# Attention scores on four quarters of the TensorE array, in a kernel of retention attention and two feed-forward layers

## The chip, the core and the metric

One core of one Trainium2 chip runs the whole program. The metric is the device time of one execution in microseconds (us), as the median of the runs. The engines that matter are TensorE (PE in the profile; its weight loads are PEld), VectorE (DVE), ScalarE (ACT), GpSimd (POOL) and SyncE (SP), whose queue issues most transfers.

## The reference

For each of 4 batches and 8 heads there are 576 positions with 64 features. Scores between queries and keys are multiplied by a decay that falls with the distance and is zero ahead of the query, and then by the values:

```python
scores = scale * np.matmul(q, k.transpose(0, 1, 3, 2))
gamma = 1.0 - 2.0 ** (-5.0 - np.arange(H))
Dmat = np.where(rel >= 0, gamma[:, None, None] ** rel[None, :, :], 0.0)
ret = scores * Dmat[None, :, :, :]
x = np.matmul(ret, v)                    # then (2304 tokens, 512)
h = x @ w_in;  x = (np.maximum(h, 0) + alpha * np.minimum(h, 0)) @ w_out
h = x @ w_in2; y = (h / (1 + np.exp(-1.702 * h))) @ w_out2
```

Both feed-forward layers are 512 to 2048 to 512 over 2304 tokens. All is computed in float32.

## The kernel before, in words

The attention works on 16 pairs of heads, one after the other. A pair has its two heads on the two halves of the partitions: features 0 to 63 of head `e` = 0 on partitions 0 to 63, of head 1 on 64 to 127 (`halves`, L300). The 576 positions are four chunks of 128 and a tail of 64. Since the decay is a power of the distance, only the scores inside a chunk are formed; what lies before a chunk comes in through a 64 by 64 state for each head.

For pair `i`, TensorE does five things, in this order, which the loop from L950 writes out by hand:

- `a_scores(i)` (L363): for each chunk `j` and head `e`, keys (64 by 128, the weights) times queries (64 by 128, moving), into the bank `t[e]` of the tile `sc`. Two PSUM banks are used, one for each head; three of them rotate. VectorE multiplies them by the decay table in `a_evac(i)` (L385).
- `a_outer(i)`: the states of the chunks, from scaled keys (`kts`) and values, into `st`. ScalarE scales these keys in `a_keys` (L317), once they have landed from HBM.
- `a_within(i-1)`: values times decayed scores of the pair before, into `av`.
- `a_tail(i)`: the scores of the tail, into `st`.
- `a_across(i-1)`: the states times queries of the pair before, into the same `av`.

All of these go through the helper `mm` (L353), so that they share one line in the profile and are told apart by the tile that they write: `sc`, `st` or `av`. An instruction that has 64 rows of weights uses one half of the array's rows, one with 64 columns one half of its columns. In the profile's notation rows*columns, the scores are 64*128, `a_outer` and `a_within` 128*64, `a_tail` and `a_across` 64*64 (there on two of the four quarters, head 0 on the upper left and head 1 on the lower right).

Each float32 product of the program stands in the trace as two weight loads and two matmuls: 8 products of scores in a pair are x16.

Loads: `a_load(i+4)` is issued on SP's queue at the end of pair `i`, when the buffer of an older pair is free: 864 KB of queries, keys and values (tile `ld`) and 256 KB of keys in the other layout (tile `kts`). Pieces of the first layer's weights (tile `raw`, 512 KB each) are issued between them, at times that a list of events sets in units of pairs (`row`, `at`, `run_to`). ScalarE and VectorE then work on these weights between the attention's own work, in the order in which the program was written: `w_sat` (L133), `w_range` (L137), `w_top` (L141) and, on VectorE, `w_low` (L148). Each engine runs its list in order.

The feed-forward layers that follow take TensorE from 66.5 us to the end. They are not touched.

Of the kernel before, what the change touches and what calls it, by code (L numbers as in the profile page):

```python
# [46 lines left out]
def kernel(  # L47
# [252 lines left out]
    halves = (slice(0, 64), slice(64, 128))  # L300
# [51 lines left out]
    def mm(out, lhsT, rhs, start, stop):  # L352
        return nc.tensor.matmul(  # L353
            out=out, lhsT=lhsT, rhs=rhs, start=start, stop=stop, skip_group_check=True
        )
# [7 lines left out]
    def a_scores(i, chunks=range(4)):  # L363
        q, k = ld[i][0:2]
        if i not in sc_t:
            sc_t[i] = [aps.tile([128, 512], F32, tag="sc", name="sc", bufs=3) for _ in halves]
        t = sc_t[i]
        for j in chunks:
            for e, o in enumerate(halves):
                mm(t[e][:, j * 128:j * 128 + 128], k[j][o], q[j][o], j == 0, True)  # L370

    def a_tail(i):
        q, k = ld[i][0:2]
# [552 lines left out]
    with tc.manual_schedule():  # L926
# [24 lines left out]
        for i in range(n_a + 1):  # L951
            j = i - 1
            if i < n_a:
                a_scores(i)
                a_queries(i)
                a_evac(i)
# [84 lines left out]
        for r in range(R):  # L1041
            z = r * 2 * NU
            for j in range(NJ):
                u = z + 7 * j
                for t, what in (
# [3 lines left out]
                    if r == 0 and j in (5, 6) and what in ("g22", "g12"):  # L1049
                        t = 8.01  # L1050
# [114 lines left out]
```

## Time and profile before

| what | value |
|---|---|
| median of 3 runs (lowest to highest) | 801.3 us (800.87 to 804.2) |
| the profiled execution | 800.28 us, of which its span is 798.6 us |
| PE busy in the span | 793.6 us (99%) |
| DVE, ACT busy | 642.1 us (80%), 527.9 us (66%) |
| granted TensorE clock | 1.00 in every stretch listed |
| HBM traffic | 267 GB/s over the span |

The chain of waits goes back from the last instruction to what released each; its rows in order of time give a start, a duration and the work, in us. In a matmul group, the shape rows*columns is that of the weights and the next one that of the moving operand. A matmul's own duration is longer than the distance between two starts, since they are pipelined: rates are read from a stage's duration divided by its instructions.

### The profile page before, as it was taken

What the parts mean: (1) busy time and instruction counts of PE and PEld (TensorE: products, weight loads), DVE (VectorE), ACT (ScalarE), POOL (GpSimd) and SP (SyncE); (2) the same over time, 40 slices, a digit from 0 to 9 for tenths busy, and PEclk for the clock granted to TensorE, in tenths of its full rate; (3) what the DMA queues carried; (4) which work ended last, traced back from release to release, by engine and by line L of the source; (5) the groups of instructions that cost most, each with busy time, mean ns of one, the idle gap of its engine ahead of it and who ended that gap; (6) DMA issues with size and microseconds to landing.
All of it is one profiled execution on the core that took longest, in us unless ns stands there. A gap on an engine that the chain in (4) does not pass through costs nothing.

```text
span 798.6 us, 14132 instructions
## 1 busy us (share of the span) xinstructions
PE 793.6 (99%) x5004; PEld 740.2 (93%) x5004; DVE 642.1 (80%) x1195; ACT 527.9 (66%) x959; POOL 83.5 (10%) x104
## 2 busy tenths in 40 slices
PE   9999999999999999999999999999999999999998
PEld 8998888888888888999999999999999999999997
DVE  7888987888467576879999899799677898787775
ACT  7689869885536856556678666676566675666552
POOL 2230112100022003626100000000000000000000
PEclk9999999999999999999999999999999999999999
DMA  9998999755889966797989556986435985536771
GB/s 351 417 386 333 327 352 342 286 217 209 294 278 401 360 224 227 253 337 254 337 323 355 177 174 233 343 295 235 147 125 193 323 312 187 159 120 232 267 278 60
DMA packets 87789, 214.08 MB, mean 268 GB/s; under 512 B 7971, under 2 KB 43811, under 8 KB 79014
## 3 DMA queue, kind: packets, MB, share of 16 engines
q1 hardware_dynamic: 80784, 187.99, 65.6%
q0 software_dynamic: 6784, 25.17, 9.0%
q8 instruction: 39, 0.64, 0.3%
q14 instruction: 32, 0.26, 0.1%
q10 hardware_dynamic: 150, 0.02, 0.0%
HBM read 152.59 MB, written 60.56 MB: 267 GB/s over the span
## 4 chain that ended last, share of the span: by engine, by line
PE 98%; DMA 1%; DVE 0%; issue 0%
PE acc L696 33%; PE h L696 25%; PE acc L555 16%; PE h L514 16%; PE av L353 4%; PE sc L353 2%; PE st L353 2%; DMA ws<-sm 1%; PE wps L942 0%; PE dq L326 0%; DVE c L178 0%; DVE wz L930 0%
## 5 line engine op out<-in xcount | busy, mean ns | idle before, releaser
L108 DVE TENSOR_TENSOR gsf<-g,gsf 128x384 fp32r<-128x384 f32 (+1 forms) x272 | 156.4, 586 | 54.5 <-ACT gsf L103 53.1
L103 ACT ACTIVATE gsf<-g 128x384 fp32r<-128x384 f32 (+1 forms) x272 | 145.8, 542 | 75.6 <-PE acc L696 32.8
L555 PE MATMUL acc<-gsf,wo 128*128 128x512 f32 x576 | 138.2, 389 | 0.0
L514 PE MATMUL h<-x,wi 128*128 128x512 f32 x576 | 138.2, 389 | 0.0
L696 PE MATMUL acc<-gsf,ws 128*128 128x384 f32 x768 | 135.1, 334 | 0.2 <-DMA ws<-sm 0.2
L696 PEld LDWEIGHTS acc<-gsf,ws 128*128 128x128 f32 x768 | 133.2, 188 | 0.5 <-ACT x L103 0.5
L555 PEld LDWEIGHTS acc<-gsf,wo 128*128 128x128 f32 x576 | 108.1, 188 | 22.8 <-ACT raw L103 0.3
L514 PEld LDWEIGHTS h<-x,wi 128*128 128x128 f32 x576 | 108.1, 188 | 22.5
L696 PE MATMUL acc<-x,ws 128*128 128x384 f32 x660 | 128.3, 334 | 0.0
L696 PEld LDWEIGHTS acc<-x,ws 128*128 128x128 f32 x660 | 115.5, 188 | 0.2 <-ACT tm L103 0.2
L696 PE MATMUL h<-x,ws 128*128 128x384 f32 x540 | 107.7, 334 | 0.0
L696 PE MATMUL h<-gsf,ws 128*128 128x384 f32 x576 | 101.9, 334 | 0.0
L696 PEld LDWEIGHTS h<-gsf,ws 128*128 128x128 f32 x576 | 100.0, 188 | 0.2 <-issue 0.2
L696 PEld LDWEIGHTS h<-x,ws 128*128 128x128 f32 x540 | 94.8, 188 | 0.0
L178 DVE TENSOR_TENSOR tm<-h,tm 128x384 f32<-128x384 f32 x97 | 53.6, 553 | 26.9 <-PE h L696 21.5
L178 DVE TENSOR_TENSOR g<-g 128x384 f32<-128x384 f32 x114 | 63.0, 553 | 0.7
L103 ACT ACTIVATE tm<-acc 128x384 f32<-128x384 f32 x62 | 30.4, 491 | 48.0 <-PE acc L696 46.4
L522 DVE SCALAR_TENSOR_TENSOR g<-g,rise_sb,h 128x512 f32<-128x512 f32 (+1 forms) x49 | 36.4, 742 | 29.7 <-ACT g L527 29.5
L527 ACT ACTIVATE g<-h 128x512 f32<-128x512 f32 (+1 forms) x49 | 29.1, 593 | 40.5 <-PE h L514 39.9
L178 DVE TENSOR_TENSOR raw<-raw 128x256 f32<-128x256 f32 x116 | 45.6, 433 | 1.0
L148 DVE SCALAR_TENSOR_TENSOR raw<-raw 128x1024 int32<-128x1024 int32 x32 | 39.3, 1229 | 2.6 <-ACT raw L141 2.6
L129 POOL DMA_DIRECT2D raw<-in_w_dram x44 | 23.2, 534 | 173.2 <-DVE raw L178 52.9
(104 smaller groups left out, 922.9 us busy)
## 6 DMA issues: line engine op xcount, KB each, us to landing
ws<-sm SPq DMA_DIRECT2D x32, 1024.0 KB, 7.0
ws<-sp SPq DMA_DIRECT2D x24, 1024.0 KB, 5.5
raw<-in_w_dram POOLq DMA_DIRECT2D x44, 512.0 KB, 7.5
sm<-raw SPq DMA_DIRECT2D x32, 512.0 KB, 4.3
pad<-rg SPq DMA_DIRECT2D x48, 256.0 KB, 2.7
ld<-in_qkv_dram SPq DMA_DIRECT2D x13, 864.0 KB, 7.9
raw<-in_w_dram SPq DMA_DIRECT2D x20, 512.0 KB, 8.9
r<-raw SPq DMA_DIRECT2D x16, 512.0 KB, 2.9
```

Source lines behind the costliest of these rows:

```text
L103: return nc.scalar.activation(out=out, in_=in_, func=ACTF.Copy)
L108: latest[0] = eng.tensor_tensor(out=out, in0=a, in1=b.bitcast(F32), op=ALU.subtract)
L129: eng.dma_start(out=raws[key][:, c * DM:c * DM + DM], in_=f[:, c * DM:c * DM + DM])
L148: latest[0] = nc.vector.scalar_tensor_tensor(out=g[:, 0:2 * DM], in0=t[:, :, 1], scalar=3, in1=t[:, :, 0], op0=ALU.logical_shift_left, op1 ...
L178: latest[0] = (eng or nc.vector).tensor_tensor(out=out, in0=x, in1=y, op=op)
L353: return nc.tensor.matmul(out=out, lhsT=lhsT, rhs=rhs, start=start, stop=stop, skip_group_check=True)
L514: nc.tensor.matmul(out=t, lhsT=w[:, cw, k * 128:k * 128 + 128], rhs=x[:, cx], start=(i == 0), stop=(i == 3 * NK - 1),)
L522: nc.vector.scalar_tensor_tensor(out=g[0], in0=g[1], scalar=rise_sb[:, m:m + 1], in1=h, op0=ALU.mult, op1=ALU.add)
L527: nc.scalar.activation(out=out, in_=in_, func=ACTF.Relu, scale=-1.0)
L555: nc.tensor.matmul(out=acc[0][d], lhsT=w[:, d // 2, cw, d % 2 * 128:d % 2 * 128 + 128], rhs=g[:, cx], start=(m == m0 and i == 0), stop=(m ...
L696: nc.tensor.matmul(out=out, lhsT=w(cw), rhs=x(cx), start=(start and n == 0), stop=True, skip_group_check=True,)
```

## The change

The weights of each score product are cut into two halves of 64 keys (`h`). Half `h` writes partitions `h` of the bank `t[e]` that held all 128 keys before. A score product then uses one quarter of the array: rows by the head `e`, columns by the half `h`. A chunk has four products where it had two, and each streams the same 128 queries.

```diff
         for j in chunks:
-            for e, o in enumerate(halves):
-                mm(t[e][:, j * 128:j * 128 + 128], k[j][o], q[j][o], j == 0, True)
+            for h in halves:
+                for e, o in enumerate(halves):
+                    mm(t[e][h, j * 128:j * 128 + 128], k[j][o, h], q[j][o], j == 0, True)
```

On TensorE, around the scores of a pair in the middle of the attention, this stood before (the shape is that of the output; `av<-r,ld` with 64x64 ends `a_across`, `st<-ld,kts` is `a_outer`, `av<-r,ld` with 64x128 is `a_within`, the last `st<-ld` is `a_tail`):

```order
L353 MATMUL av<-r 64x128 x6
L353 MATMUL av<-r 64x64 x2
L353 MATMUL av<-r,ld 64x64 x2
L353 MATMUL sc<-ld 128x128 x8
L353 MATMUL st<-ld,kts 64x64 x8
L353 MATMUL av<-r,ld 64x128 x8
L353 MATMUL st<-ld 64x64 x2
```

and this stands now:

```order
L353 MATMUL av<-r 64x128 x6
L353 MATMUL av<-r 64x64 x2
L353 MATMUL av<-r,ld 64x64 x2
L353 MATMUL sc<-ld 64x128 x16
L353 MATMUL st<-ld,kts 64x64 x8
L353 MATMUL av<-r,ld 64x128 x8
L353 MATMUL st<-ld 64x64 x2
```

The eight products became sixteen of half the output, in the same place; nothing around them moved.

Inside a pair the two heads take turns. With the numbers of the tiles, the scores of one pair (`sc_524` for head 0, `sc_525` for head 1) and what stands behind them were, before:

```order
L353 MATMUL sc_524<-ld_342 128x128
L353 MATMUL sc_525<-ld_342 128x128
L353 MATMUL sc_524<-ld_342 128x128
L353 MATMUL sc_525<-ld_342 128x128
L353 MATMUL st_539<-ld_342,kts_127 64x64 x8
```

The last two chunks of a pair and what stands behind them are now, with other numbers of the tiles (`sc_572` for head 0, `sc_573` for head 1):

```order
L353 MATMUL sc_572<-ld_366 64x128
L353 MATMUL sc_573<-ld_366 64x128
L353 MATMUL sc_572<-ld_366 64x128
L353 MATMUL sc_573<-ld_366 64x128
L353 MATMUL sc_572<-ld_366 64x128
L353 MATMUL sc_573<-ld_366 64x128
L353 MATMUL sc_572<-ld_366 64x128
L353 MATMUL sc_573<-ld_366 64x128
L353 MATMUL st_595<-ld_366,kts_127 64x64 x8
```

The heads alternate as before, and the two products of one head that are nearest are the two halves of one chunk's keys. On DVE, ACT, POOL and SP the instructions and their order are unchanged.

## Rows read from the trace of the kernel before

**Rows 1.** The page: busy time of TensorE, and the chain that ended last.

```profile
PE 793.6 (99%) x5004; PEld 740.2 (93%) x5004; DVE 642.1 (80%) x1195; ACT 527.9 (66%) x959; POOL 83.5 (10%) x104
...
PE acc L696 33%; PE h L696 25%; PE acc L555 16%; PE h L514 16%; PE av L353 4%; PE sc L353 2%; PE st L353 2%; DMA ws<-sm 1%; PE wps L942 0%; PE dq L326 0%; DVE c L178 0%; DVE wz L930 0%
```

**Rows 2.** The chain in order of time, one pair: start us, us, what.

```profile
55.86 0.26 PE st L353 x4
56.12 0.89 PE av L353 x20
57.01 1.09 PE sc L353 x16
58.10 0.61 PE st L353 x16
58.72 0.88 PE av L353 x16
```

**Rows 3.** The timeline of PE around 57.00 and 58.60: start us, us, what.

```profile
56.94 0.38 PE L353 MATMUL sc<-ld 64*128 64x128 f32 x2
...
58.55 0.28 PE L353 MATMUL av<-r,ld 128*64 128x128 f32 x2
```

**Rows 4.** Tiles `sc` (20 to 60 us) and `av` (58.5 to 59.4): ns min/median/max.

```profile
L353 PE MATMUL sc<-ld x174: 272/272/373, 19.8 to 57.8; 64*128 64x128 f32 x174
...
L353 PEld LDWEIGHTS av<-r,ld x16: 137/137/138, 58.5 to 59.2; 128*64 128x64 f32 x16
L353 PE MATMUL av<-r,ld x16: 272/273/275, 58.5 to 59.3; 128*64 128x128 f32 x16
```

**Rows 5.** Groups on PE by form, first 200 us: busy us, mean ns, idle.

```profile
L353 PE MATMUL sc<-ld 64*128 64x128 f32 x256 | 19.5, 294 | 0.0
L353 PE MATMUL av<-r,ld 128*64 128x128 f32 x256 | 17.1, 275 | 0.0
L353 PE MATMUL av<-r 64*64 64x128 f32 x192 | 13.2, 270 | 0.0
```

**Rows 6.** Stretches: PE, PEld, DVE, ACT, POOL busy, PEclk, DMA share, GB/s.

```profile
8.00:20.00 12.00, 12.00 (x224) 10.80 (x223) 11.77 (x31) 10.11 (x29) 4.58 (x4) 1.00 1.04 416
...
30.00:40.00 10.00, 10.00 (x199) 9.09 (x197) 7.95 (x18) 9.34 (x19) 2.45 (x3) 1.00 1.03 420
...
66.00:100.00 34.00, 34.00 (x161) 27.85 (x158) 29.12 (x47) 31.12 (x43) 3.81 (x7) 1.00 0.88 317
```

**Rows 7.** The timeline of ACT in the fourth pair.

```profile
16.02 0.91 ACT L317 ACTIVATE kts<-kts,vtab_sb 128x256 f32<-128x256 f32 x2 [0.57 <-DMA kts<-in_kn_dram]
```

**Rows 8.** The chain in order of time, the fourth pair.

```profile
15.71 1.09 PE sc L353 x16
16.80 0.80 PE st L353 x15
17.60 0.93 PE av L353 x16
```

**Rows 9.** The timeline of SP's queue, 31.3 to 35.2 us.

```profile
31.38 0.38 SPq L311 DMA_DIRECT2D kts<-in_kn_dram  x1
31.81 0.42 SPq L129 DMA_DIRECT2D raw<-in_w_dram  x1
```

**Rows 10.** DMA issues at 31.4 us: KB each, us to landing.

```profile
kts<-in_kn_dram SPq DMA_DIRECT2D x1, 256.0 KB, 7.9
```

**Rows 11.** The timeline of ACT, 37.5 to 43 us.

```profile
37.55 0.53 ACT L317 ACTIVATE r<-st,vtab_sb 128x320 f32<-128x320 f32 x1 [0.49 <-issue]
37.98 0.90 ACT L317 ACTIVATE kts<-kts,vtab_sb 128x256 f32<-128x256 f32 x2
...
40.54 1.18 ACT L133 ACTIVATE raw<-raw 128x1024 f32<-128x1024 f32 x1
41.60 0.52 ACT L317 ACTIVATE r<-st,vtab_sb 128x320 f32<-128x320 f32 x1
42.00 0.91 ACT L317 ACTIVATE kts<-kts,vtab_sb 128x256 f32<-128x256 f32 x2
```

**Rows 12.** The chain in order of time, the eleventh pair.

```profile
42.08 1.09 PE sc L353 x16
43.17 0.61 PE st L353 x16
```

## The prediction

> **What bounds the kernel now.** I read the page first, for which engine ends the chain: PE is busy 99% of the span and nearly the whole chain of waits runs through its lines; of the lines, the scores (`sc`) are 2%, about 16 us [rows 1]. So a microsecond off PE counts, unless the next instruction on PE then waits for someone else. The chain in order of time shows that inside a pair PE goes from stage to stage without a break: `a_tail` 0.26, `a_across` 0.89, the scores 1.09, `a_outer` 0.61, `a_within` 0.88, in all 3.73 us a pair [rows 2]. Then I read the stretches, for what else is near its limit: the DMA share is above 1.0 at 416 to 420 GB/s up to 40 us, and ACT is busy 9.34 of 10 us between 30 and 40 us [rows 6]. These two decide how much of a saving survives.
>
> **What a round of products costs.** In the timeline, the first two matmuls of the scores fill 0.38 us together, while the longest single one lasts 373 ns; the first two of `a_within` fill 0.28 us and each lasts 275 ns [rows 3, 4]. So the two halves of the array start within some 7 ns and run beside each other, split by rows (scores) as by columns (`a_within`); by their mean durations alone, 294 and 275 ns, one would not see it [rows 5]. I call such a pair a round. `a_within` has 16 matmuls with 128 moving columns in 0.88 us: 8 rounds of 0.110 us [rows 2]. It stands behind `a_outer`, which uses the same tiling. `a_across` stands behind `a_tail`, again of the same tiling, and holds 6 rounds of 128 and 4 of 64 columns, 6 x 0.110 + 4 x 0.055 = 0.88 of its 0.89 us [rows 2]. The three stages that follow a different tiling are longer than their rounds: the scores 1.09 - 8 x 0.110 = 0.21 us, `a_outer` 0.61 - 8 x 0.055 = 0.17 us, `a_tail` 0.26 - 2 x 0.055 = 0.15 us. I read this as the price of entering another tiling: 0.15 to 0.21 us, with about 0.2 us ahead of the scores.
>
> **The change, part by part.**
> It removes one entry. The scores become 64*64, as `a_across` ahead of them; behind them `a_outer` is 128*64 and pays its entry as before. Worth 0.21 us a pair; at the least nothing, if quarters other than the two that `a_across` uses have to be entered too.
>
> It doubles the score instructions, 16 matmuls to 32 in a pair, each still with 128 moving columns. If all four quarters run beside each other these are 8 rounds as before. No stage of this kernel runs four at once, so I bound the round. From below 0.110 us, the round of two. From above two rounds one after the other, 0.220 us: then the scores take 16 x 0.110 = 1.76 us. Between these lies the pace of issue and weight loads: `a_outer` gets through 16 loads of 64 columns and 16 matmuls in 0.61 us with its entry, 0.038 us each; four of them are 0.152 us a round and 1.22 us a stage. Without the entry it is 0.44 us, 0.0275 each, 0.110 a round. I take 0.110, nearest to the rows that show each split alone at full pace: rows and columns are each independent [rows 3, 4], 32 loads of 64 columns hold as many columns as 16 of 128 did, and four moving streams over 64 partitions read no more than the two over 128 of `a_within`. The stage then takes 0.88 us, 0.21 less: 16 x 0.21 = 3.4 us at most.
>
> VectorE waits for the last product of a bank, which is still among the last two of the stage; its work, the banks and all the other queues are as before.
>
> **How much of it stays on the path.** First, pairs 0 to 3. In the fourth pair ACT waits 0.57 us for the landing of `kts` and scales these keys from 16.02 to 16.93 us [rows 7]; PE's `a_outer` there takes 0.80 instead of 0.61 [rows 8]: it already waits. That transfer was in a queue with a DMA share of 1.04 from 8 to 20 us [rows 6], and it does not land sooner because PE is sooner. What the first four pairs save, 0.8 us, becomes a longer wait at this place. Twelve pairs are left, 12 x 0.21 = 2.5 us.
>
> Second, a weight piece. ACT works in order. At 40.54 us it starts on a `raw` whose second piece was issued at 31.81 us, right behind a `kts` issued at 31.38 us that landed 7.9 us later, at 39.3 us [rows 9, 10, 11]. The trace has no landing for that piece; 512 KB at the 420 GB/s of this stretch [rows 6] after 39.3 us give an estimate of 40.5 us. So this start has almost no slack. Behind it on ACT stand the state of that pair and the keys of the next, finished at 42.91 us, and PE's `a_outer` of pair 10 began at 43.17 us [rows 11, 12], 0.26 us later. By then PE would be 7 x 0.21 = 1.5 us ahead (pairs 4 to 10), and ACT about as much, but the piece lands when it lands. ACT waits, PE waits for the scaled keys, and the lead shrinks to 0.26 + 0.04 = 0.3 us. The price is 1.2 us.
>
> Third, pairs 11 to 15: 5 x 0.2 = 1.0 us, with later pieces well ahead of their use. At the end of the attention PE is 0.3 + 1.0 = 1.3 us ahead. From 66 us PE is busy 34.00 of 34.00 us with a DMA share of 0.88 [rows 6]; I let the lead stand to the end, since what PE waits for there is mostly work that PE itself releases.
>
> The sum is -1.3 us. Against the profiled execution that is 800.28 - 1.3 = 799.0 us. The median of the runs, 801.3, stands 1.0 us above that execution; I start from halfway, 800.8, and predict 799.5 us.
>
> **A rule that speaks against it.** In `a_within`, whose two streams share all 128 rows, each load lasts 137 ns and still 16 loads and 16 matmuls fit into 0.88 us: loads are hidden under the matmuls of the other column half [rows 2, 4]. The Trainium skill, "TensorE: Matmul & The Clock Gate", Part 3 (The mechanism), says that a weight load overlaps a running matmul only when its row group is another one. Here two quarters of a head share their rows. By that rule their loads would be exposed (rival 3 gives its time from rows); by the row they stay hidden. The same part of that page gives a 10.6-fold gain for 16 tiles split both ways, in another type and with longer streams; no run here shows it.
>
> **The rivals.**
> 1. The saving arrives nearly whole: the weight piece lands a microsecond sooner than I estimate, and only the first four pairs lose theirs: 800.8 - 2.5 = 798.3 us. For it: the landing is not in the trace. Against: ACT began on that piece with 0.04 us to spare by the estimate.
> 2. Quarters that share a head's rows take turns: the two halves of a chunk's keys need the same 64 partitions of queries as moving operand, at their own times, and if only one stream at a time can enter a row half, a pair has 16 rounds of 0.110 us. The stage takes 1.76 us, 0.67 more, on PE with nothing to hide it: 16 x 0.67 = 10.7 us, 811.5 us. It decides as soon as a round of four takes longer than 1.09 / 8 = 0.136 us. For it: no row has two streams in one row half of the array. Against: `a_within` has two streams on the same 128 partitions at full pace. A partial form is the 0.152 us round: +0.13 a pair, +2.1 us, 802.9 us.
> 3. Loads between quarters of the same rows are not hidden: 16 rounds, each with the 0.15 us that an entry costs, 16 x 0.26 = 4.2 us a stage, 3.1 more, some 850 us. Against it stands the row above.
> 4. The change does not do what it says, because the four quarters are entered anew behind `a_across`: rounds as forecast and the entry as before, 800.8 us.
>
> **How the numbers follow.** Forecast 0.58; rival 1 0.14; rival 4 0.05; the partial form 0.06; rival 2 0.14; rival 3 0.03. What a measurement here can tell from no change is about 0.5%, 4.0 us. The largest saving worked out, 3.4 us, lies below that, so faster gets 0.02, for luck of the run alone. Slower holds rivals 2 and 3 and a part of the partial form: 0.18. The rest, 0.80, is no change that can be told. The range goes from 800.8 - 3.4 = 797.4 us, all of it saved, to 804.0 us, the median plus the partial form and a little scatter; rivals 2 and 3 are left out. The forecast's own range is 798.0 to 801.5 us.
>
> **What would show it.** The chain rows of a pair: scores at 0.88 to 0.93 us for x32, `a_outer` still 0.61, `a_across` still 0.89. If the scores stand at 1.76, rival 2 holds; at 1.22 its partial form; at 1.09, rival 4. In the fourth pair, `a_outer` should end at about 17.6 us as before, and ACT's wait for `kts` grow. Near 40.5 us ACT should show a new wait of about 1 us ahead of L133, and PE one ahead of the `a_outer` of pair 10; the first feed-forward matmul should start about 1.3 us sooner than 66.5. If that wait is missing and the start is 2.5 us sooner, the weight piece was mis-sized. If the attention ends sooner but the span doesn't, my step that the lead stands to the end is wrong.

## The result, and the profile after

The changed kernel takes 808.62 us (median of 6 runs, 806.46 to 809.87) against 801.49 us (6 runs): a ratio of 1.0077, 95% interval 1.0054 to 1.0101. That is 7.1 us slower; forecast was 799.5 us, with 804.0 us as the upper end. The profiled execution is 809.11 us with a span of 807.4 us.

The scores themselves did what was forecast. The chain of the changed kernel in order of time (start us, us, what), a pair and the stages around it (two of the 32 score matmuls run beside the row ahead):

```profile
22.95 0.26 PE st L353 x4
23.21 0.83 PE av L353 x18
24.10 0.88 PE sc L353 x30
24.98 0.62 PE st L353 x16
25.59 0.65 PE av L353 x11
26.24 0.37 issue
26.61 0.54 PE av L353 x5
```

The scores stand at 0.88 us for 32 matmuls, against 1.09 us for 16 in [rows 2]; `a_outer` behind them is as long as before. The entry is gone so thoroughly that the first scores run beside the last matmuls of `a_across`. In the timeline of PE (start us, us, engine line op, tiles, shapes) two of them start ahead of two matmuls of `a_across` that the program has before them:

```profile
60.19 0.32 PE L353 MATMUL sc<-ld 64*64 64x128 f32 x1
60.19 0.22 PE L353 MATMUL av<-r,ld 64*64 64x64 f32 x1
60.19 0.32 PE L353 MATMUL sc<-ld 64*64 64x128 f32 x1
60.24 0.22 PE L353 MATMUL av<-r,ld 64*64 64x64 f32 x2
60.30 1.04 PE L353 MATMUL sc<-ld 64*64 64x128 f32 x29
63.72 0.32 PE L353 MATMUL sc<-ld 64*64 64x128 f32 x1 [2.38 <-issue]
```

The loss is in the last row here and in the one called "issue" above: TensorE stands still and waits for nothing that the profile shows. Before, no such wait stood in the attention's chain. Now there are six, from the chain between 24 and 63.8 us:

```profile
26.24 0.37 issue
...
32.25 0.27 issue
...
37.64 1.44 issue
...
49.76 0.51 issue
...
56.03 0.42 issue
...
61.33 2.38 issue
```

Where do they stand? Neither at one stage nor at one pair, but at even distances in TensorE's own list. The stretches from one stall to the next hold (columns as in [rows 6]; the third spans two distances):

```profile
26.40:32.40 6.00, 5.64 (x127) 4.88 (x128) 4.14 (x11) 3.21 (x9) 1.14 (x1) 1.00 1.03 409
32.40:38.50 6.10, 5.12 (x127) 4.46 (x127) 4.38 (x11) 5.70 (x11) 2.29 (x2) 1.00 0.99 368
38.50:50.00 11.50, 10.68 (x255) 9.51 (x254) 8.86 (x19) 9.23 (x18) 2.84 (x3) 1.00 0.98 356
50.00:56.20 6.20, 5.76 (x127) 5.01 (x128) 4.15 (x9) 3.14 (x7) 1.76 (x2) 1.00 1.02 408
56.20:62.50 6.30, 4.88 (x128) 4.29 (x127) 4.82 (x11) 6.13 (x11) 2.13 (x2) 1.00 0.99 304
```

That is 127 or 128 matmuls and as many weight loads each time, about 256 instructions, or twice that. Counted with the few semaphore instructions that TensorE's list also holds, the instruction behind every one of the six stalls has the same number modulo 256; the text calls these places borders, by the numbers 961, 1217, 1473, 1985, 2241 and 2497. Of the DMA queues on the page of the profile (packets, MB, share of 16 engines), one carries instructions and has grown with TensorE's list. In the kernel before:

```profile
q8 instruction: 39, 0.64, 0.3%
```

In the changed kernel:

```profile
q8 instruction: 41, 0.67, 0.3%
```

0.67 MB in 41 packets is 16 KB a packet, and 5260 matmuls with 5260 loads over 41 packets are 257 instructions a packet. The two packets more are the 512 instructions more. Read packet by packet, the trace gives this, in us (entered: when TensorE starts on a block of 256; the packet that begins next carries the block behind it; late: the distance of the starts across the border, where 0.0 is no stall):

```
kernel   entered   packet begins, ends    next block starts   late
before    24.01     27.06   27.99           30.49              0.0
before    56.78     59.27   60.15           63.42              0.0
after     20.80     24.40   25.35           26.61              0.6
after     32.52     36.75   37.63           39.08              1.7
after     56.45     61.53   62.49           63.71              2.7
```

At all six stalls TensorE goes on 1.2 to 1.6 us after the packet's end. Before, a block lasted 6.4 to 6.8 us and its successor had landed 2.5 to 4.0 us before it was needed, 1 to 2.5 us more than those 1.2 to 1.6. The changed kernel has 176 instructions in a pair of 3.52 us and would use a block up in 256 / 176 x 3.52 = 5.1 us, and at the six stalls the next one could be started only 5.7 to 7.3 us after the last was entered. The packets themselves also began later than before: with the latest begin of the kernel before, 3.3 us after a block was entered, 1.0 us for the packet and those 1.2 to 1.6 us, a border would be late by 0.4 to 0.8 us. The delays of 1.7 and 2.7 us follow packets that began 4.2 and 5.1 us after. Why they began so late at the same DMA share, no run separates.

A long stall has a second price. The granted clock in the stretches behind the longest one:

```profile
61.30:63.70 2.40, 0.03 (x1) 0.00 (x0) 0.69 (x1) 1.29 (x2) 1.15 (x1) 1.00 1.03 394
63.70:67.00 3.30, 3.29 (x45) 2.83 (x47) 2.12 (x5) 0.46 (x2) 0.00 (x0) 0.68 1.05 431
67.00:70.00 3.00, 3.00 (x72) 2.83 (x70) 1.62 (x5) 2.60 (x5) 1.15 (x1) 0.79 0.97 365
```

The seventh column after the stretch falls to 0.68 and 0.79 as means: TensorE ran at 1.2 GHz for a part of them, after 2.4 us of standing still. The chain has the price there:

```profile
64.65 1.39 PE av L353 x16
66.04 0.41 PE st L353 x4
66.45 1.59 PE av L353 x17
```

Against 0.88, 0.26 and 0.83 us these are 1.4 us.

### The profile page after: what moved, and what is told of

It is laid out like the page before. It is cut to its first block, busy times and chain, and to the rows that moved or that the text cites. A ratio compares the mean times of both kernels' runs of the same rounds, so it can differ in the third digit from the quotient of the medians.

```text
span 807.4 us, 14644 instructions
## 1 busy us (share of the span) xinstructions
PE 795.0 (98%) x5260; PEld 739.9 (92%) x5260; DVE 642.6 (80%) x1195; ACT 528.9 (66%) x959; POOL 83.8 (10%) x104
## 4 chain that ended last, share of the span: by engine, by line
PE 89%; DMA 4%; DVE 3%; issue 1%; SPq 1%; ACT 1%; DVEq 0%; POOLq 0%; ACTq 0%
PE acc L697 32%; PE h L697 25%; PE acc L556 13%; PE h L515 13%; PE av L353 4%; PE sc L353 2%; PE st L353 2%; DMA raw<-in_w_dram 1%; DMA rg<-raw 1%; DMA ws<-sp 1%; DMA ld<-in_qkv_dram 1%; SPq L498 1%; DVE raw L198 1%; DMA x<-part 0%; DVE g L523 0%
```

## The experiments

Theory F: TensorE's instructions arrive in blocks of 256, the fetch takes longer where the DMA engines are full, and the additional instructions use a block up before the next is there. Theory Q, the rival: quarters themselves bring the loss, whatever the number of instructions.

**Quarters in the odd pairs only.**

```diff
-            for h in halves:
+            for h in halves if i % 2 else (slice(0, 128),):
```

> Quarters in the odd pairs only, halves in the even ones. Theory F (instruction blocks): TensorE's instructions arrive in blocks of 256; in the changed kernel each block arrives about 5 to 7 us after TensorE has entered the block before, and TensorE uses one up in 4.4 us, so it stands still at block borders (numbers 961, 1217, 1473, 1985, 2241, 2497 of its instructions). With 176 instructions a pair on average a block lasts 5.3 us unstalled: some borders still stall, about 1 to 3 us in all, against 8 x 0.2 us saved. 800 to 803 us, stalls only at those borders (same numbers mod 256). Theory Q (the quarters themselves cost time wherever they are used): half of the loss of 7.1 us, 805 us, stalls tied to the odd pairs.

Measured: 802.39 us against 801.55, ratio 1.0009 (0.9993 to 1.0024). F holds: a block lasts 5.8 us unstalled (160 instructions a pair on average; the expectation had miscounted 176, and 4.4 us a block in the changed kernel where 5.1 us is right), four borders are late, by 0.2, 0.2, 1.5 and 1.2 us, all at the same numbers modulo 256, and the loss is far from half of 7.1 us.

**Less traffic, with quarters and with halves.** From pair 5 on, one edit in both kernels:

```diff
-        t = tmp("ld", i, [128, 1728])
+        t = kept_ld[i % 5] if i > 4 else tmp("ld", i, [128, 1728])
+        kept_ld[i % 5] = t
```

> The changed kernel, but from pair 5 on the tile with queries, keys and values of the pair five before is used again and not loaded (864 KB a pair less; its values are then not the reference's). Theory F with fetches slowed by full DMA engines: a block arrives in under 4.4 us, the stalls at borders after pair 5 go, TensorE's pairs last 3.5 us, and it ends 2 to 3 us ahead of the same cut in the kernel before. Theory F with a fixed fetch time: the stalls stay, 0.4 to 1.5 us at each border. Theory Q: the loss of some 7 us against the same cut before stays.

> The kernel before with the same cut: from pair 5 on the tile of queries, keys and values of five pairs before is used again and not loaded. It is the other half of the comparison. All theories: no stalls at borders, 3.73 us a pair, about 798 to 801 us; TensorE was not waiting for these loads.

Measured: 800.43 us with quarters and 801.71 us with halves, both against 801.55; ratios 0.9988 (0.9977 to 0.9998) and 1.0001 (0.9990 to 1.0011). Without the loads, the same quarters are not slower but by the medians 1.3 us faster than the same halves, where 2 to 3 us were expected; the two intervals overlap a little, so that this gain is less sure than the end of the loss. The stretches with quarters:

```profile
20.00:30.00 10.00, 9.46 (x244) 8.37 (x242) 8.16 (x21) 5.50 (x15) 3.63 (x4) 1.00 1.04 412
30.00:40.00 10.00, 9.73 (x237) 8.62 (x234) 7.71 (x16) 8.14 (x16) 2.83 (x3) 1.00 0.56 199
40.00:50.00 10.00, 10.00 (x246) 8.93 (x238) 8.10 (x19) 9.16 (x17) 3.46 (x3) 1.00 0.15 56
```

The borders near 26 us, at a DMA share of 1.04, and 32 us are late by 0.8 and 0.5 us. After that the share falls to 0.56 and 0.15 on average, from 40 us PE is busy 10.00 of 10.00 us, and no border is late any more: the next packets begin from 0.5 us before to 1.9 us after a block is entered, where it was 3.6 us. So the fetch is not of a fixed length; it queues with the data. Its gain over the halves is smaller than 16 x 0.21 = 3.4 us: two borders were late, and in two later pairs `a_outer` takes 0.78 and 0.72 us instead of 0.61.

**Quarters without additional instructions.**

```diff
-        for j in chunks:
+        for j in (0, 2):
...
-                    mm(t[e][h, j * 128:j * 128 + 128], k[j][o, h], q[j][o], j == 0, True)
+                    mm(t[e][h, j * 128:j * 128 + 256], k[j][o, h], ld[i][3][o, j * 64:j * 64 + 256], j == 0, True)
```

> Quarters without additional instructions: only the keys of chunks 0 and 2 are used as weights, in quarters, and each streams 256 queries instead of 128 (8 products as in the kernel before; the scores are then not the reference's). The scores' stage has the length of the changed kernel's, 0.88 us, its tiling, and no entry, with 144 instructions a pair as before. Theory F: a block lasts 6.3 us, longer than its fetch, no stalls at borders; what the prediction said holds: -1 to -2.5 us against before, 798.5 to 800.5 us. Theory Q: the stalls and the loss stay, 806 to 809 us.

Measured: 800.49 us against 801.55, ratio 0.9981 (0.9969 to 0.9993): 1.5 us faster by the ratio, 0.6 to 2.5 us. No border is late in the attention. A pair in its chain:

```profile
53.24 0.87 PE sc L353 x14
54.11 0.61 PE st L353 x16
54.73 0.88 PE av L353 x16
55.60 0.26 PE st L353 x4
55.86 0.82 PE av L353 x17
56.69 0.06 PE sc L353 x2
```

Four quarters, full DMA engines (a share of 1.02 from 20 to 50 us), 144 instructions a pair: 3.51 us a pair and no stall. Q falls. From the first matmul of `a_outer` in pair 1 to the first of the feed-forward layers this kernel takes 54.2 us (11.73 to 65.95), the one before 56.3 us (10.14 to 66.46) and the changed one 62.7 us (11.11 to 73.78).

**The instructions without quarters.** In the kernel before, `a_within` in two streams:

```diff
-                mm(av_t[i][1][j][o], v[:, 2 * j + e], r[:, e, j * 128:j * 128 + 128], j % 2 == 0, True)
+            for c in (0, 64):
+                for e, o in enumerate(halves):
+                    mm(av_t[i][1][j][o, c:c + 64], v[:, 2 * j + e],
+                       r[:, e, j * 128 + c:j * 128 + c + 64], j % 2 == 0 and c == 0, True)
```

> The kernel before (scores on halves) with a_within in two streams of 64 columns each instead of one of 128: the same work for the array (16 rounds of 0.055 us instead of 8 of 0.110), the same tilings, no quarters in the scores, but 32 more instructions of TensorE in a pair, 176 instead of 144, as many as the changed kernel has. (The expectation of the run with odd pairs took 208 and 176 a pair; the counts are 176 for the changed kernel and 160 with odd pairs, so that a block of 256 lasts 5.1 and 5.8 us there.) Theory F: a block lasts 5.4 us unstalled and arrives some 6 us after the one before is entered: stalls at the borders (numbers 961, 1217, ... as in the changed kernel), 4 to 6 us slower than before, 805 to 807 us. Theory Q (quarters in the scores are what costs): no stalls, 801 to 802 us.

Measured: 808.05 us against 801.15, ratio 1.0073 (1.0048 to 1.0097): the whole loss, with scores on halves. Who waited on PE in this kernel (us in total, times, longest):

```profile
PE st L353 <- issue: 2.0, 1, 2.0
PE av L353 <- issue: 1.9, 2, 1.3
...
PE sc L353 <- issue: 0.2, 1, 0.2
```

The stalls stand at other stages, but at the same numbers of instructions (961, 1473, 2241 and 2497, and the next of the row, 2753). The expectation of 805 to 807 us was too low by a microsecond. Two of its borders were late by 2.2 and 1.5 us, and the granted clock was 0.83 on average between 40 and 50 us, behind the first of them; the estimate had no term for the clock.

**The changed kernel again.**

> The changed kernel once more, for a second profile. Theory F: the stalls stand at the same numbers of TensorE's instructions, their lengths differ, 806 to 810 us. If the wait of 1.1 us near 257 us for the split of g by ACT comes again, it belongs to the change; if not, to that execution.

Measured: 810.55 us (2 runs). Five borders are late, at five of the six numbers of the first profile, by 1.1, 2.0, 1.4, 0.7 and 3.8 us. The 1.1 us for which PE waited near 257 us in the first profile, with `acc` behind `gsf`, is not there, so it belonged to that execution.

**Quarters in four pairs, twice, and the kernel before again.**

```diff
-            for h in halves:
+            for h in halves if i in (4, 6, 8, 10) else (slice(0, 128),):
```

> Quarters in pairs 4, 6, 8 and 10 only, where the run with odd pairs showed hardly a stall (0.2 us up to instruction 1729). Theory F: a block lasts at least 5.8 us there, the stalls stay below 0.3 us, and 4 x 0.2 us are saved: 0.5 to 0.8 us faster than before, 800.7 us, not to be told from no change. Theory Q: 4 of 16 pairs bring a quarter of the loss, +1.8 us, 803.3 us.

Measured: 802.98 us against 801.15, ratio 1.0017 (1.0008 to 1.0026): a miss, and where Q had expected it. The profile doesn't show Q's loss: from instruction 193 to the feed-forward layers it takes 56.0 us, as before, with borders late by 0.1 to 0.4 us that eat most of the saving. Most of the excess lies ahead: instruction 193, in `a_outer` of pair 1, starts at 12.86 us against 10.54 in the first profile of before, and up to there the two programs are the same. So both ran once more:

> The kernel before once more, for a second profile of its first 13 us. If the first transfers land late in some executions of any kernel, its pair 0 may begin its states at 6.6 us as in the first profile or at about 7.5 us as in the profile with four quartered pairs; either is compatible with 800.5 to 804 us.

> Quarters in pairs 4, 6, 8 and 10 once more. Its first profile was 2.3 us late before the first quartered pair, with hardly a stall after it. Theory start (the miss of 1.8 us is the late start, which has nothing to do with quarters): a late start again with 802 to 804 us, or an early one with 800.5 to 801.5 us. Theory Q: an early start and still 802.5 to 803.5 us.

Measured: 801.67 us for the kernel before, whose instruction 193 now starts at 11.50 us, and 801.39 us for the sparse quarters, with 11.80 us and 55.6 us from there on. The start differs from execution to execution without any change: the third piece of the first `ld` landed at 6.64 us in one profile of before and at 7.40 us in the late one of the sparse kernel, and the chain of before shows in its second profile that a late start is also a slow one (start us, us, what; the first profile had 1.06 and 1.09 us):

```profile
8.11 1.82 PE av L353 x16
9.93 1.23 PE sc L353 x16
```

In the late profile of the sparse kernel the same scores took 2.01 us. How long TensorE stays at this slow pace differs from execution to execution; why, no run shows. Whether the sparse kernel starts late more often than the one before, and why, stays open: the interval of its 12 runs, 1.0008 to 1.0026, leaves out 1, and its profiles have no loss of that size behind the start. In no case is there a gain.

## Why the prediction was wrong, point by point

- **A round of four at 0.110 us: right.** 0.88 us for eight rounds. The Trainium skill, "TensorE: Matmul & The Clock Gate", Part 3 (The mechanism), lets weight loads hide only under another row group; quarters of a head share rows. Each quarter has 8 matmuls of 0.110 us and so streams through all of the 0.88 us, and the loads of the other quarter in its rows fall into that time: 0.88 us leaves no room for exposed loads. The trace disagrees with the rule for quarters as it did for column halves.
- **One entry less, 0.21 us: right**, shown by the rows with 0.88 us and by 3.51 us a pair in the run without additional instructions.
- **What it adds.** Here the prediction failed. It bounded the pace of issue by a stage of 0.6 us, 0.0275 to 0.038 us for a load and its matmul, found 32 more instructions a pair free of charge, and held that all the other queues are as before. It left out that the list of instructions itself has to be brought in, by a queue that carries 41 packets where it carried 39. Over a whole block TensorE had used 256 instructions in 6.4 to 6.8 us; now it would use them in 5.1 us, and at the late borders the next block could be started only 5.7 to 7.3 us after the last was entered. So the term that stood at nothing measured 7.0 us of late borders and 1.4 us of slower clock. With 176 instructions in 3.52 us the supply, not the array, sets the time. The DMA share of 1.0 of [rows 6], which I held only against the data, makes it so: at shares of 0.56 and less no border was late.
- **The account.** Between `a_outer` of pair 1 and the feed-forward layers the changed kernel lost 62.7 - 56.3 = 6.4 us. The starts across the six late borders add up to 7.0 us, the slower clock behind the longest stall costs 1.4 us, and the saving of the run without additional instructions was 56.3 - 54.2 = 2.1 us: 7.0 + 1.4 - 2.1 = 6.3 us. That closes to what such rows can tell. The rest of the 8.8 us between the two profiled spans is a start some 1.0 us later and some 1.5 us in the feed-forward layers, 1.1 us of it the wait near 257 us that did not come again.
- **-1.3 us on the path**, where the supply holds: the run without additional instructions gave -1.5 us (-2.5 to -0.6). That the two agree is in part luck, as the largest deduction, 1.2 us for a weight piece, was not seen. Two reasons for less than 3.4 us were seen, the first one forecast: from instruction 193 to the scores of pair 4 that run gained 0.1 us only, and `a_outer` waited 0.2 us for keys in pairs 8, 10 and 14 (0.83, 0.78 and 0.76 us instead of 0.61). The forecast wait of ACT for a weight piece near 40.5 us was not tested: that execution began 1.6 us late, and ACT came to that piece at 41.1 us without a wait.
- **The rivals.** None held. Rivals 2 and 3 (quarters that take turns, loads that are exposed) had the right sign for a reason that the rows of the scores exclude; that rival 2's 811.5 us lies near the 808.6 us measured is chance.

## What to carry to other kernels

A change that splits products to fill the array multiplies instructions, so hold the new number per microsecond against the supply: here 256 in about 6 us while the DMA engines were full, and the kernel before was already within 1 to 2.5 us of that limit. In a profile the sign is a wait named "issue" at even distances in the engine's own count, wherever in the program that falls; the run that settles it adds the instructions and nothing else. A saving of 0.2 us a pair that costs 32 instructions a pair was no bargain; the same tiling at the old count was, though here only in a kernel whose scores are not the reference's.

## What the runs showed of the hardware that was not expected

- TensorE's instructions came in packets of 16 KB, 256 instructions. A packet began 1.3 to 3.3 us after a block was entered in the kernel before and 2.0 to 6.0 us after in the two profiles of the changed one at full DMA engines, but from 0.5 us before to 1.9 us after at mean shares of 0.15 to 0.56; TensorE went on 1.2 to 1.6 us after the packet's end at every stall.
- Matmuls can overtake earlier ones: two of the scores started at 60.19 us, ahead of two of `a_across` at 60.24 us that stand before them in the program. `a_across` leaves two quarters free, and the early scores are presumably those on the free ones; the trace does not name the quarter.
- All four 64 by 64 quarters ran at the full pace of two halves, in float32: 32 matmuls of 128 columns in 0.88 us.
